# A joint Winograd level for one product of the gate and up projections, and sums of DFT blocks made by DMA

## The chip, the cores and the metric

The kernel runs on one core of a Trainium2 chip. The metric is the device time of one execution in microseconds. It is one launch; the arrays are laid out by the host beforehand and lie in HBM.

## What is computed

For x of 2048 rows and 512 columns, all in float32, the kernel mixes two branches:

```python
a = x @ hid_re.T;  b = x @ hid_im.T
y = seq_re @ a - seq_im @ b                  # Fourier mixing, real part
h = relu(x @ W_gate) * (x @ W_up)            # 512 -> 1792 columns
g = sigmoid(sum(x * gate_w, -1))
out = g * y + (1 - g) * (h @ W_down)
```

## The kernel before

**Arithmetic.** Every float32 operand is split into a high part `hi` and a low part `lo` of type float32r: ScalarE (ACT) makes `hi` by a cast, VectorE (DVE) makes `lo` by a subtraction. One product is three matmuls of 128x512 in PSUM: lo x hi, hi x lo, hi x hi (`PARTS`, line 366). Above that, matrix products are taken as 2x2 blocks with seven products instead of eight (Winograd). `LEFT` and `RIGHT` (lines 25, 26) name for each product 1 to 7 the blocks or sums that it multiplies: product 1 is block 11 by block 11, product 2 is block 12 by block 21. The eight PSUM banks are four pairs x, m, y, t, and `BANK` (line 29) says to which pair each product adds up.

**Gate and up.** W_gate and W_up are taken in seven column pairs c = 0 to 6, the rows of x in two halves q = 0, 1. One `Block` (line 493) is one c and one q: seven products, each for gate and up (i = 0, 1), each of 2 x 3 matmuls, 84 in all. After product 1 ACT copies pair x to pair y (line 542), so that both sums go on from it; products 5 and 6 are copied to SBUF as `s5`, `s6` (line 544); after products 2, 7, 3 and 4 the four blocks of h are finished on ACT and DVE (`rectified`, `added`, lines 528 to 539). `h_out` (line 474) makes the four sums of h that the down projection needs (`hs`) and stores h and the sums to `hd` in HBM.

**Order of the stages.** The blocks of c = 0 and 1 for q = 0 are interleaved at the start, product by product (lines 1006 to 1017; product 1 and 2 of the first block only are cut into shorter steps). Then come c = 2 to 6 with both halves, the spectral stage (x times the hidden DFT, results to `ad`), two remaining blocks of q = 1, `Down` (the down projection, twice), `Sequence` and `Joint` (the sequence DFT). `Joint` makes, for one of the two DFT matrices, products whose right sides are sums of DFT blocks; `joint_sums` (line 934) has made these ahead: each of its four calls loads four blocks of 512 KB (`jt`) on SyncE's DMA queue (SP), adds them pairwise on DVE (128x1024), and stores four results to `td` in HBM on GpSimd's queue (POOL).

**What sets the order.** Each operation is given a key, the number of matmuls planned ahead of it. `Plan` (line 129) works out when each is due and when its inputs are ready by its own table of costs, and lists DVE, ACT, SP and POOL in that order; TensorE (PE) keeps the written order. Each engine then runs its list in order. Loads go through SP; stores, and DMAs that add to their destination (`accumulate`), through POOL. SBUF is 51 equal units that buffers take in turn, so the first writer of a buffer waits for the last reader of the one before in its unit, a DMA included.

Of the kernel before, what the change touches and what calls it, by code (L numbers as in the profile page):

```python
# [14 lines left out]
P = 128  # L15
# [263 lines left out]
def kernel(ctx: ExitStack, tc, xP, xG, wgu, wd, cr, ci, wri, gw, out):  # L279
# [80 lines left out]
    def store(o, i):  # L360
        plan.gpsimd.dma_start(out=o, in_=i)

    def accumulate(o, i):
        plan.gpsimd.dma_start(out=o, in_=i, accum_op=OP.add)
# [9 lines left out]
    def x_load(q, b, ks=slice(0, 2), at=None):  # L374
        k, j = int(b[0]) - 1, int(b[1]) - 1
        (at or load)(piece[q, b][:, ks], xP[2 * q + j, k, :, ks])
# [6 lines left out]
    def x_sum(q, m):  # L383
        if len(RIGHT[m]) > 1:
            a, b = ((piece[q, n] if isinstance(n, str) else X[q, n][2]).all for n in RIGHT[m][:2])
            combine(X[q, m][2].all, a, b, RIGHT[m][2])
# [7 lines left out]
    def x_prep(q, m, key):  # L394
        x_raw(q, m)
        op(key, x_sum, q, m)
        op(key + 7, hi_of, X[q, m])
        op(key + 12, lo_of, X[q, m])
# [75 lines left out]
    def h_out(q, c, h, key):  # L474
        f = [buf(f"hs{n}") for n in range(2)]

        def first():
            e = E()
            e.vector.tensor_add(f[0][:, 0], h[0][:, 0], h[0][:, 1])
            e.vector.tensor_add(f[0][:, 1], h[0][:, 1], h[1][:, 1])  # L480

        def second():
            e = E()
            e.vector.tensor_add(f[1][:, 0], f[0][:, 0], h[1][:, 1])
            e.vector.tensor_add(f[1][:, 1], f[1][:, 0], h[1][:, 0])

        op(key, first)
        op(key + 6, second)
        op(key + 2, lambda: store(hd[q, 0, :, c], h[0][:, 0]))
        for n, t, k in ((1, h[1], 3), (3, f[0], 8), (5, f[1], 14)):  # L490
            op(key + k, lambda n=n, t=t: store(hd[q, n:n + 2, :, c].rearrange("x p n -> p x n"), t.all))

    class Block:


        def __init__(self, q, w, banks=PAIRS):
            self.q, self.w, self.banks = q, w, banks
            self.g = {r: buf("g" + r, (N,)) for r in ("11", "21")}
# [11 lines left out]
        def done(self, key):  # L510
            h_out(self.q, self.w.c, self.h, key)
# [6 lines left out]
        def one(self, m, i, k, n, first=0):  # L518
            w, x, ps = self.w.of(m, i, k), X[self.q, m], self.banks[BANK[m]]
# [4 lines left out]
        def evac(self, m, key):  # L524
# [11 lines left out]
            def added(r, ps, s):  # L536
                u, h = self.u[r], self.h[int(r[0]) - 1][:, 1]
                op(key, lambda: e.vector.tensor_add(u.all, ps.all, s.all))
                op(key + 1, lambda: e.vector.scalar_tensor_tensor(h, u[:, 0], 0.0, u[:, 1], op0=OP.max, op1=OP.mult))
# [12 lines left out]
            elif m == 4:  # L552
                rectified("21", 0, t, -1.0)

# [59 lines left out]
    class SpectralBlock:  # L614
        def __init__(self, sp, q, ih):
            self.sp, self.q, self.ih = sp, q, ih
            self.s = {m: buf(f"s{m}") for m in (5, 6)}
# [8 lines left out]
        def product(self, m, i):  # L626
            x, w, ps = X[self.q, m], self.sp.w[m], PAIRS[BANK[m]]
# [215 lines left out]
    class Joint:  # L843


        HI, LO = 31, 24
# [40 lines left out]
        def right(self, x, hh, key):  # L887
# [9 lines left out]
            op(key - 90, read)  # L897
# [64 lines left out]
    def x_half(m, k, hi=None):  # L962
        h, l, raw = (t[:, k] for t in X[0, m])
# [8 lines left out]
    for k in halves:  # L972
        op(-99, x_load, 0, "11", k)
        op(-99, ws[0].load, 0, halves[0], k)
    op(-99, ws[1].load, 0, halves[0])
    op(-99, x_load, 0, "21")
    for w in ws:
        op(-99, w.load, 0, halves[1])
    op(-98, x_load, 0, "12")
    for w in ws:  # L980
        op(-98, w.load, 1)
    op(-98, x_load, 0, "22")
    op(-98, lambda: load(gwt[:], gw))
    for k in halves:
        op(-90, x_half, 1, k, plan.vector.tensor_copy)
        op(-90, w_half, ws[0], halves[0], k)
    op(-90, w_half, ws[1], halves[0])
    op(-90, x_half, 2, halves[0])
    op(-90, w_half, ws[0], halves[1])
    op(-90, x_half, 2, halves[1])  # L990
    op(-90, w_half, ws[1], halves[1])
    for n, m in enumerate((5, 6, 3, 7, 4)):
        key = 24 * n + 20
        for f, *a in ((x_sum, 0, m), (hi_of, X[0, m]), (lo_of, X[0, m])):
# [12 lines left out]
    for m in ORDER_S:  # L1007
        for b in start:
            if m in (1, 2) and b is start[0]:
# [8 lines left out]
    for b in start:  # L1018
        b.done(plan.now + 100)
# [27 lines left out]

    blocks(sequence)
# [104 lines left out]
```

## Time and profile before

| | us |
|---|---|
| median of the runs (lowest, highest) | 790.61 (789.64, 792.07) |
| profiled execution | 789.88 |
| its span, first to last instruction | 788.1 |
| outside the span | 1.8 |
| PE busy, 3435 matmuls | 780.7 |
| DVE busy | 620.4 |
| ACT busy | 390.4 |
| POOL busy | 96.1 |

PE here is TensorE's matmuls, PEld its weight loads. The granted clock of TensorE was 0.999 over the span. In the chain of the work that ended last, each row is a start, a length and the instructions that ran in that time; in the list of waits the numbers are the total, how often, and the longest. Of a DMA, busy time counts only the issue, and "landing" is the time from issue until the data are there.

### The profile page before, as it was taken

How to read it: one execution, taken by the hardware profiler on the slowest of the kernel's cores; microseconds unless marked ns; L12 is line 12 of the kernel's file. 1: busy time of each engine (PE TensorE's matmuls, PEld its weight loads, DVE VectorE, ACT ScalarE, POOL GpSimd, SP SyncE). 2: the span in 40 equal slices, each digit the busy share in tenths (PEclk: the TensorE clock that was granted, in tenths of full speed). 3: DMA queues.
4: the chain of work that ended last, by engine and by line, in shares of the span. 5: the costliest groups of instructions: out<-in, count | busy, mean ns of one | idle time of the engine just before them, and what ended most of it. 6: DMA issues, size and time to landing. Idle time of an engine off the chain costs nothing.

```text
span 788.1 us, 9404 instructions
## 1 busy us (share of the span) xinstructions
PE 780.7 (99%) x3435; PEld 644.7 (82%) x3435; DVE 620.4 (79%) x663; ACT 390.4 (50%) x436; POOL 96.1 (12%) x142
## 2 busy tenths in 40 slices
PE   9999999999999999999999999999999999999997
PEld 7888888888888888888888888888888888888885
DVE  7999676667688314978764899967999999989963
ACT  6664333333354335476545464545757365574540
POOL 0011221212122111110000000200020001000200
PEclk9999999999999999999999999999999999999999
DMA  8354775576867975477688798859999889799914
GB/s 324 128 202 166 290 291 214 218 262 242 282 225 233 364 314 184 131 257 293 191 267 315 279 306 311 196 184 294 355 328 270 252 255 188 197 351 330 240 30 81
DMA packets 56574, 193.84 MB, mean 246 GB/s; under 512 B 6608, under 2 KB 6864, under 8 KB 56528
## 3 DMA queue, kind: packets, MB, share of 16 engines
q1 hardware_dynamic: 37552, 124.55, 45.2%
q0 software_dynamic: 18976, 68.69, 29.6%
q8 instruction: 27, 0.44, 0.2%
q14 instruction: 19, 0.16, 0.1%
HBM read 123.99 MB, written 60.83 MB: 235 GB/s over the span
## 4 chain that ended last, share of the span: by engine, by line
PE 97%; ACT 1%; issue 1%; DMA 1%; DVE 0%; SPq 0%; DVEq 0%
PE ps L126 97%; ACT jch L126 1%; DMA wr<-wgu 1%; SPq L126 0%; DVE v L126 0%; DVE z L126 0%; ACT js L126 0%; DVE wal L126 0%; ACT wah L126 0%; ACT ps L126 0%; DVEq L126 0%
## 5 line engine op out<-in xcount | busy, mean ns | idle before, releaser
L126 PE MATMUL ps<-ch,ll 128*128 128x512 f32 x580 | 225.6, 389 | 0.0
L126 PE MATMUL ps<-cl,lh 128*128 128x512 f32 x580 | 225.6, 389 | 0.0
L126 PE MATMUL ps<-ch,lh 128*128 128x512 f32 x580 | 225.6, 389 | 0.0
L126 ACT CAST ch<-r 128x1024 fp32r<-128x1024 f32 x96 | 97.4, 1052 | 72.5 <-DVE r L126 59.9
L126 PEld LDWEIGHTS ps<-ch,lh 128*128 128x128 f32 x580 | 108.9, 188 | 22.7
L126 PEld LDWEIGHTS ps<-ch,ll 128*128 128x128 f32 x580 | 108.9, 188 | 22.7
L126 PEld LDWEIGHTS ps<-cl,lh 128*128 128x128 f32 x580 | 108.9, 188 | 22.4
L126 DVE TENSOR_TENSOR cl<-r,ch 128x1024 fp32r<-128x1024 f32 x96 | 114.6, 1222 | 1.2 <-ACT ch L126 0.6
L126 ACT ACTIVATE ps<-ps 128x1024 f32<-128x1024 f32 (+1 forms) x34 | 32.6, 958 | 87.5 <-PE ps L126 41.0
L126 DVE TENSOR_TENSOR cl<-hr,ch 128x1024 fp32r<-128x1024 f32 (+1 forms) x56 | 59.3, 1088 | 20.4 <-ACT ch L126 18.6
L126 ACT COPY s<-ps 128x1024 f32<-128x1024 f32 x44 | 44.6, 1014 | 52.8 <-PE ps L126 52.8
L126 ACT CAST ch<-hr 128x1024 fp32r<-128x1024 f32 (+1 forms) x56 | 51.3, 942 | 26.7 <-PE ps L126 20.1
L126 DVE TENSOR_TENSOR r<-r,r 128x1024 f32<-128x1024 f32 x48 | 57.2, 1221 | 0.0
L126 POOL DMA_DIRECT2D out<-z x23 | 17.1, 743 | 322.5 <-DVE z L126 322.5
L126 DVE TENSOR_TENSOR u<-ps,s 128x1024 f32<-128x1024 f32 x28 | 34.2, 1221 | 12.4 <-PE ps L126 6.9
L126 PE MATMUL ps<-xh,wb0l 128*128 128x512 f32 x112 | 43.8, 391 | 0.0
L126 PE MATMUL ps<-xl,wb0h 128*128 128x512 f32 x112 | 43.6, 389 | 0.0
L126 PE MATMUL ps<-xh,wb0h 128*128 128x512 f32 x112 | 43.6, 389 | 0.0
L126 PE MATMUL ps<-xh,wb1h 128*128 128x512 f32 x112 | 43.6, 389 | 0.0
L126 PE MATMUL ps<-vh,xh 128*128 128x512 f32 x112 | 43.6, 389 | 0.0
L126 PE MATMUL ps<-vh,xl 128*128 128x512 f32 x112 | 43.6, 389 | 0.0
L126 PE MATMUL ps<-xh,wb1l 128*128 128x512 f32 x112 | 43.6, 389 | 0.0
(126 smaller groups left out, 1311.2 us busy)
## 6 DMA issues: line engine op xcount, KB each, us to landing
hr<-hd SPq DMA_DIRECT2D x42, 512.0 KB, 4.5
r<-cr SPq DMA_DIRECT2D x32, 512.0 KB, 5.7
r<-ci SPq DMA_DIRECT2D x32, 512.0 KB, 5.8
hd<-hs POOLq DMA_DIRECT2D x28, 512.0 KB, 5.2
out<-z POOLq DMA_DIRECT2D x23, 512.0 KB, 6.4
td<-jt POOLq DMA_DIRECT2D x16, 512.0 KB, 3.9
ad<-a POOLq DMA_DIRECT2D x16, 512.0 KB, 3.9
l<-ad SPq DMA_DIRECT2D x16, 512.0 KB, 7.2
```

Of the source, the lines that this page charges most:

```text
L126: getattr(getattr(nc, self.engine), self.name)(*map(ap, self.a), **{k: ap(x) for k, x in self.k.items()})
```

## The change

**Product 2 for both halves together.** For c = 3 to 6, a `Joined` pair of blocks replaces two Blocks. Block 12 of the weights and block 21 of x for both halves form a 2x2 product again, gate and up on one side, the two halves on the other. `JointW` and `JointX` make its sums, splits and seven steps of three matmuls: 21 in place of 24. `JointX` is prepared once (seven casts, eleven DVE operations of 128x512), `JointW` once per pair (four DVE operations of 128x128, a cast and a subtraction of 128x512). The steps run in pair x inside the q = 0 block, and their results reach SBUF as `jv` (ACT copies) and `jo` (DVE adds, one ACT copy), 128x512 each. For that, product 1 of the q = 0 block goes to pair y and is copied to `s1`, and the block "11" of h is made from `s1` or pair x plus `jo` by DVE (`u11`).

**Sums by DMA.** `joint_sums` makes the sums without SBUF: POOL copies a block from HBM into `td` in HBM and then adds a second block by an accumulating DMA. Two of the four sums start from a sum already in `td`. All 32 DMAs have 512 KB in pieces of 1 KB.

**Further edits.** At the start, products 1 and 2 of both blocks are cut into the short steps. The sums of h for c = 0, 1, q = 0 are made in the spectral stage from a reloaded h (`h_late`), and block 21 of x is reloaded and split again for that stage. x of the second half is prepared at a spacing of 24 instead of 27, and the right sides of `Joint` are loaded, cast and split a little later.

The core of the diff:

```diff
-    def h_out(q, c, h, key):
+    def h_sums(q, c, h, key):
...
+        for n, t, k in ((3, f[0], 8), (5, f[1], 14)):
+            op(key + k, lambda n=n, t=t: store(h_forms(q, c, n), t.all))
+
+    def h_forms(q, c, n):
...
+    def h_out(q, c, h, key, sums=True):
+        if sums:
+            h_sums(q, c, h, key)
         op(key + 2, lambda: store(hd[q, 0, :, c], h[0][:, 0]))
-        for n, t, k in ((1, h[1], 3), (3, f[0], 8), (5, f[1], 14)):
-            op(key + k, lambda n=n, t=t: store(hd[q, n:n + 2, :, c].rearrange("x p n -> p x n"), t.all))
+        op(key + 3, lambda: store(h_forms(q, c, 1), h[1].all))
+        if not sums:
+            op(key + 2, lambda: store(hd[q, 3, :, c], h[0][:, 1]))
+
+    def h_late(q, c, key):
+        h = [buf(f"hk{d}") for d in range(2)]
+        for i, n in enumerate((0, 3)):
+            op(key - 20 + i, lambda i=i, n=n: load(h[0][:, i], hd[q, n, :, c]))
+        op(key - 18, lambda: load(h[1].all, h_forms(q, c, 1)))
+        h_sums(q, c, h, key)
...
+        def added(self, r, a, b, key):
+            u, h = self.u[r], self.h[int(r[0]) - 1][:, int(r[1]) - 1]
+            op(key, lambda: E().vector.tensor_add(u.all, a.all, b.all))
+            op(key + 1, lambda: E().vector.scalar_tensor_tensor(h, u[:, 0], 0.0, u[:, 1], op0=OP.max, op1=OP.mult))
+    class Joined(Block):
+        def __init__(self, q, w):
+            super().__init__(q, w)
+            self.u["11"] = buf("u11")
+            if not q:
+                self.s[1] = buf("s1")
+        def run(self, joint=None):
+            slots = {(1, 1): (5, 1), (6, 1): (6,), (3, 0): (3, 7), (3, 1): (2, 4)}
+            for m, i in (*((m, i) for m in ((1, 5) if self.q else (5, 1)) for i in range(2)), (6, 0), (6, 1), (3, 0), (7, 0), (7, 1), (3, 1), (4, 0), (4, 1)):
+                pe(6, self.product, m, i)
+                if i:
+                    self.evac(m, plan.now)
+                for y in slots.get((m, i), ()) if joint else ():
+                    joint.step(y)
+        def done(self, key, joint):
+            self.added("11", self.s[1] if self.q == 0 else self.banks["x"], joint.o[self.q], plan.now)
+            super().done(key)
+        def one(self, m, i, k, n):
+            w, x, ps = self.w.of(m, i, k), self.x[m], self.banks["y" if m == 1 and not self.q else BANK[m]]
+            a, b = PARTS[n]
+            mm(ps[i], w[a], x[b][:, k], start=m in FIRST and k == n == 0, stop=m in (3, 4) and k == 1 and n == 2)
+        def evac(self, m, key):
+            y, t = self.banks["y"], self.banks["t"]
+            if m == 1 and not self.q:
+                op(key, lambda: E().scalar.copy(self.s[1].all, y.all))
+            elif m == 7:
+                for i in range(2):
+                    op(key, lambda i=i: E().scalar.activation(t[i], y[i], AF.Copy, scale=-1.0))
+                self.added("22", y, self.s[5], key)
+            else:
+                super().evac(m, key)
+    class JointX:
+        def __init__(self, key):
+            a, b = (piece[q, "21"] for q in range(2))
+            raw = [buf(f"jx{n}") for n in range(2)]
+            t5, t6, t7, t4 = raw[0][:, 0], raw[0][:, 1], raw[1][:, 0], raw[1][:, 1]
+            self.x = {}
+            for n, (y, src, f) in enumerate((
+                    (1, a[:, 0], None), (5, t5, (b[:, 0], a[:, 0])), (6, t6, (b[:, 1], t5)), (3, b[:, 1], None),
+                    (7, t7, (b[:, 1], b[:, 0])), (2, a[:, 1], None), (4, t4, (a[:, 1], t6)))):
+                x = self.x[y] = buf(f"jx{y}", dtype=F32R)
+                if f:
+                    op(key + 16 * n, lambda src=src, f=f: combine(src, *f, -1))
+                op(key + 16 * n + 4, lambda x=x, src=src: E().scalar.copy(x[:, 0], src))
+                op(key + 16 * n + 8, lambda x=x, src=src: E().vector.tensor_sub(x[:, 1], src, f32(x[:, 0])))
+    class JointW:
+        def __init__(self, w, x, key):
+            self.w, self.x = w, x
+            raw, s = buf("jws", [4, P]), w.raw[0]
+            self.t = buf("jw", [2, 4, P], F32R)
+            self.s = {y: buf(f"jv{y}", (N,)) for y in (1, 5, 6)}
+            self.o = [buf(f"jo{q}") for q in range(2)]
+            op(key - 30, lambda: combine(raw[:, 0], s[:, 1, 0, 1], s[:, 1, 1, 1], 1))
+            op(key - 30, lambda: combine(raw[:, 2], s[:, 1, 0, 0], s[:, 1, 0, 1], -1))
+            op(key - 29, lambda: combine(raw[:, 1], raw[:, 0], s[:, 1, 0, 0], -1))
+            op(key - 28, lambda: combine(raw[:, 3], s[:, 1, 1, 0], raw[:, 1], -1))
+            op(key - 24, lambda: E().scalar.copy(self.t[:, 0], raw.all))
+            op(key - 20, lambda: E().vector.tensor_sub(self.t[:, 1], raw.all, f32(self.t[:, 0])))
+        def left(self, y, a):
+            if y in (1, 2, 4):
+                return self.w.a[a][:, 1, int(y > 1), int(y == 4)]
+            return self.t[:, a, {5: 0, 6: 1, 7: 2, 3: 3}[y]]
+        def step(self, y):
+            pe(3, self.product, y)
+            self.evac(y, plan.now)
+        def product(self, y):
+            for n, (a, b) in enumerate(PARTS):
+                mm(PAIRS["x"][int(y in (5, 3, 2))], self.left(y, a), self.x.x[y][:, b],
+                   start=y in (1, 5, 2) and n == 0, stop=n == 2)
+        def evac(self, y, key):
+            Y, M = (PAIRS["x"][n] for n in range(2))
+            s, o, e = self.s, self.o, E()
+            if y in (1, 5, 6):
+                op(key, lambda: e.scalar.copy(s[y].all, M if y == 5 else Y))
+            elif y == 4:
+                op(key, lambda: e.scalar.copy(o[0][:, 1], Y))
+            else:
+                q, i, ps, t = {3: (1, 0, M, 6), 7: (1, 1, Y, 5), 2: (0, 0, M, 1)}[y]
+                op(key, lambda: e.vector.tensor_add(o[q][:, i], ps, s[t].all))
...
-        HI, LO = 31, 24
+        HI, LO = 26, 20
...
-            op(key - 90, read)
+            op(key - 82, read)
...
-        r = {b: buf(f"jt{b}") for b in BLOCKS}
-        for n, b in enumerate(("11", "12", "22", "21")):
-            op(key + 8 * n, lambda b=b: load(r[b].all, (cr, ci)[m][2 * int(b[1]) - 2, 1, 2 * int(b[0]) - 2 + hh]))
-        for n, (o, i) in enumerate((("11", "12"), ("12", "22"), ("22", "11"), ("21", "22"))):
-            op(key + 40 + 8 * n, lambda o=o, i=i: combine(r[o].all, r[o].all, r[i].all, 1))
-            op(key + 46 + 8 * n, lambda o=o, n=n: store(td[m, n, hh], r[o].all))
+        def c(b):
+            return (cr, ci)[m][2 * int(b[1]) - 2, 1, 2 * int(b[0]) - 2 + hh]
+        for n, (o, first, second) in enumerate(((0, "11", "12"), (1, "12", "22"), (2, 0, "22"), (3, 2, "21"))):
+            op(key + 30 * n, lambda o=o, i=first: store(td[m, o, hh], c(i) if isinstance(i, str) else td[m, i, hh], max_dma_last_dim=2 * N))
+            op(key + 30 * n + 15, lambda o=o, i=second: accumulate(td[m, o, hh], c(i), max_dma_last_dim=2 * N))
...
-            if m in (1, 2) and b is start[0]:
+            if m in (1, 2):
...
-        b.done(plan.now + 100)
+        b.done(plan.now + 8, False)
...
-        joint_sums(n // 2, n % 2, 380 + 160 * n)
-    sequence = [(2, 0), (2, 1)]
-    sequence += [(c, q) for c in range(3, NP) for q in range(2)]
-    tail = [(1, 1), (0, 1)]
+        joint_sums(n // 2, n % 2, 300 + 150 * n)
     spectral = Spectral()
-    def blocks(sequence):
-        nonlocal w
-        for c, q in sequence:
-            if w.c != c:
-                w = Weights(c)
-                if c == 1:
-                    w.fetch(plan.now - 140)
-                else:
-                    w_prep(w, plan.now, 66 if c else 180)
-            if c == 2 and q == 0:
-                for b in ("22", "11", "12", "21"):
-                    x_piece(1, b)
-                    op(plan.now - 100, x_load, 1, b)
-                for n, m in enumerate(ORDER):
-                    x_prep(1, m, plan.now - 46 + 27 * n)
-            Block(q, w).run()
-    blocks(sequence)
+    def prepared(c, ahead=66):
+        w = Weights(c)
+        w_prep(w, plan.now, ahead)
+        return w
+    for c in range(2, NP):
+        w = prepared(c)
+        if c == 2:
+            for b in ("22", "11", "12", "21"):
+                x_piece(1, b)
+                op(plan.now - 100, x_load(1, b))
+            for n, m in enumerate(ORDER):
+                x_prep(1, m, plan.now - 46 + 24 * n)
+            jx = JointX(plan.now + 70)
+            for q in range(2):
+                Block(q, w).run()
+        else:
+            pair = [Joined(q, w) for q in range(2)]
+            joint = JointW(w, jx, plan.now)
+            for q, b in enumerate(pair):
+                b.run(None if q else joint)
+                b.done(plan.now + 8, joint)
+    for q in range(2):
+        x_piece(q, "21")
+        op(plan.now - 150 + 60 * q, x_load(q, "21"))
+        x_prep(q, 2, plan.now - 100 + 100 * q)
...
+    for c in range(2):
+        h_late(0, c, plan.now + 30 * c)
     lefts = [spectrum(f) for f in range(2)]
     for ih in range(2):
         SpectralBlock(spectral, 1, ih)
-    blocks(tail)
+    w = Weights(1)
+    w.fetch(plan.now - 140)
+    Block(1, w).run()
+    Block(1, prepared(0, 180)).run()```

What stands on the engines at the places that matter: first TensorE's list after the change, in the q = 0 block of c = 4. The last matmuls of product 1 (`xh1`, `wah`, into pair y), then the joint steps 5 and 1 (`jx5`, `jx1`, into pair x), then product 6, which writes pair y.

```order
MATMUL ps_76<-xl1_113,wah_975 128x512
MATMUL ps_76<-xh1_107,wah_975 128x512
MATMUL ps_76<-jx5_635,jw_986 128x512 x3
MATMUL ps_76<-jx1_538,wal_994 128x512
MATMUL ps_76<-jx1_538,wah_975 128x512 x2
MATMUL ps_76<-xh6_230,wb0l_1006 128x512
```

Before, product 5 with its twelve matmuls stood between product 1 and product 6; it now runs ahead of product 1, and six joint matmuls are in its place.

Second, ScalarE's list at the same block: before the change (the copy of x to y, then of products 5 and 6, then the rectified "11" and the negated copy of product 7), and

```order
COPY ps_76<-ps_76 128x1024
COPY s5_1060<-ps_76 128x1024
COPY s6_1078<-ps_76 128x1024
ACTIVATE g11_1086<-ps_76 128x512
ACTIVATE ps_76<-ps_76 128x1024
```

after it, ScalarE's list from the cast of this pair's last weights on:

```order
CAST wd_1055<-wr1_939 128x512
COPY s5_1074<-ps_76 128x1024
COPY s1_1098<-ps_76 128x1024
COPY jv5_1107<-ps_76 128x512
COPY jv1_1112<-ps_76 128x512
COPY s6_1125<-ps_76 128x1024
COPY jv6_1132<-ps_76 128x512
ACTIVATE ps_76<-ps_76 128x512 x2
COPY jo0_1180<-ps_76 128x512
```

The copy to `s1` stands directly behind that to `s5`; three copies of joint steps are new, and the negated copy is two of 128x512.

Third, POOL's list after the change, from the stores of c = 4 on (`hd<-h`, `hd<-hs`: h and its sums) to those of c = 5, q = 0, with the copies and accumulates to `td` between them. An accumulate waits until its copy has landed, and a copy from `td` until the accumulate that made its source has.

```order
DMA td_70<-td_70 512x256
DMA hd_68<-h0_1346 128x512
DMA hd_68<-hs0_1362 128x2x512
DMA hd_68<-hs1_1371 128x2x512
DMA td_70<-ci 512x256 x2
DMA td_70<-td_70 512x256
DMA hd_68<-h0_1469 128x512
DMA td_70<-ci 512x256
DMA hd_68<-h1_1451 128x2x512
DMA td_70<-ci 512x256
DMA hd_68<-hs0_1494 128x2x512
```

Before, stores of `jt`, which waited for DVE alone, stood in these places.

More of the change, by code (lines that the diff above doesn't have):

```diff
@@ L358, in load, with store, accumulate @@
         plan.sync.dma_start(o, i)
[L360 to L364, printed above, removed]
+    def store(o, i, **k):
+        plan.gpsimd.dma_start(out=o, in_=i, **k)
+    def accumulate(o, i, **k):
+        plan.gpsimd.dma_start(out=o, in_=i, accum_op=OP.add, **k)
     PARTS = ((1, 0), (0, 1), (0, 0))
@@ L383, in x_sum @@
     def x_sum(q, m):
-        if len(RIGHT[m]) > 1:
-            a, b = ((piece[q, n] if isinstance(n, str) else X[q, n][2]).all for n in RIGHT[m][:2])
-            combine(X[q, m][2].all, a, b, RIGHT[m][2])
+        o, i = X[q, m][2], [piece[q, n] if isinstance(n, str) else X[q, n][2] for n in RIGHT[m][:2]]
+        return lambda: len(i) == 1 or combine(o.all, i[0].all, i[1].all, RIGHT[m][2])
     def hi_of(t):
@@ L497, in __init__ @@
             self.q, self.w, self.banks = q, w, banks
+            self.x = {m: X[q, m] for m in ORDER if (q, m) in X}
             self.g = {r: buf("g" + r, (N,)) for r in ("11", "21")}
@@ L508, in run, with done @@
             self.done(plan.now + (8 if plan.now > 270 else 100))
-        def done(self, key):
-            h_out(self.q, self.w.c, self.h, key)
+        def done(self, key, *sums):
+            h_out(self.q, self.w.c, self.h, key, *sums)
         def product(self, m, i):
@@ L536, in added @@
             def added(r, ps, s):
-                u, h = self.u[r], self.h[int(r[0]) - 1][:, 1]
-                op(key, lambda: e.vector.tensor_add(u.all, ps.all, s.all))
-                op(key + 1, lambda: e.vector.scalar_tensor_tensor(h, u[:, 0], 0.0, u[:, 1], op0=OP.max, op1=OP.mult))
+                self.added(r, ps, s, key)
             if m == 1:
@@ L616, in __init__ @@
             self.sp, self.q, self.ih = sp, q, ih
+            self.x = {m: X[q, m] for m in ORDER}
             self.s = {m: buf(f"s{m}") for m in (5, 6)}
```

34 lines of the change are left out of this document (18 added, 16 removed).

## The prediction

> **What bounds the kernel now.** I read the page's first table, then the chain that ended last, then what TensorE (PE) waited for.
>
> ```profile
> span 788.1 us, 9404 instructions
> PE 780.7 (99%) x3435; PEld 644.7 (82%) x3435; DVE 620.4 (79%) x663; ACT 390.4 (50%) x436; POOL 96.1 (12%) x142
> ...
> PE 97%; ACT 1%; issue 1%; DMA 1%; DVE 0%; SPq 0%; DVEq 0%
> ```
>
> PE is busy for 780.7 of 788.1 us. A busy PE alone would not prove a bound, since each matmul's record overlaps the next one; the chain does. These are its long pieces (start, length, what):
>
> ```profile
> 8.16 542.15 PE ps L126 x2387
> ...
> 555.68 0.48 ACT js L126
> ...
> 556.21 144.24 PE ps L126 x635
> ...
> 706.36 75.11 PE ps L126 x330
> ```
>
> Three unbroken runs of matmuls make 761.5 us. In the first, 542.15 / 2387 = 0.227 us per 128x512 matmul. Between the runs stand only the two Joint stages. What PE waited for confirms it:
>
> ```profile
> PE ps L126 <- DVE warm L126: 1.2, 1, 1.2
> PE ps L126 <- ACT js L126: 0.5, 2, 0.3
> PE ps L126 <- DVE wal L126: 0.4, 1, 0.4
> ```
>
> So time is the number of matmuls times 0.227 us plus about 2 us of waits. Matmuls taken away pay in full, and work on the vector engine (DVE), ScalarE (ACT) or a DMA queue costs nothing until PE waits for it.
>
> **Term 1: matmuls removed.** Each of the pairs c = 3 to 6 made product 2 in 2 halves x 2 (gate, up) x 2 x 3 = 24 matmuls of 128x512; seven products of three make 21. Four pairs save 4 x 3 = 12, and 12 x 0.227 = **-2.72 us**. Everything else in the change can only add to this or take from it.
>
> **Term 2: the copy of product 1.** In a joined pair's q = 0 block, product 1 goes to bank pair y, ACT copies y to s1, and product 6 overwrites y. Between them stand the joint steps 5 and 1: six matmuls. The same kind of copy of product 1 in the kernel before, start, length and form:
>
> ```profile
> 103.83 0.39 PE L126 MATMUL ps<-xh,wah 128*128 128x512 f32 x1
> ...
> 104.25 1.00 ACT L126 COPY ps<-ps 128x1024 f32<-128x1024 f32 x1 [3.45 <-PE ps L126]
> ...
> 555.58 0.39 PE L126 MATMUL ps<-jch,jlh 128*128 128x512 f32 x1
> 555.59 1.05 ACT L126 COPY js<-ps 128x512 f32<-128x512 f32 x2
> ...
> 556.21 0.50 PE L126 MATMUL ps<-jch,jll 128*128 128x512 f32 x1 [0.25 <-ACT js L126]
> ...
> 556.55 0.40 PE L126 MATMUL ps<-jcl,jlh 128*128 128x512 f32 x1
> ```
>
> The copy begins 104.25 - 103.83 = 0.42 us after the last matmul starts, and one into SBUF takes 1.01 us (the s<-ps row below). How fast PE resumes is read from the js stall: by the chain the copy waited for ends at 555.68 + 0.48 = 556.16, PE starts at 556.21, and its next matmul follows 0.34 us later instead of 0.227, so resuming costs about 0.05 + 0.11 = 0.16. Needed: 0.42 + 1.01 + 0.16 = 1.59 us. Available: from the start of product 1's last matmul to product 6's first are seven steps, 7 x 0.227 = 1.59. The balance is zero, so I take **0**, if ACT is free when product 1 ends. ACT then has only the s5 copy behind it, twelve matmuls (2.7 us) earlier. Should a 1.05 us cast stand in front, each pair loses up to 1.05 us, 4.2 in all. Below zero it cannot go: nothing there waited before.
>
> ```profile
> L126 ACT CAST ch<-r 128x1024 fp32r<-128x1024 f32 x96 | 97.4, 1052 | 72.5 <-DVE r L126 59.9 <-PE ps L126 7.1 <-DVE ll L126 4.0
> ...
> L126 ACT COPY s<-ps 128x1024 f32<-128x1024 f32 x44 | 44.6, 1014 | 52.8 <-PE ps L126 52.8
> ```
>
> The later joint copies and adds are 128x512, 0.57 us (js: 1.05 for two) to 0.69 us (below), and the bank each frees is next written after at least 12 more matmuls, 2.7 us: hidden.
>
> **Term 3: DVE and ACT.** DVE is the only other engine that is ever full; busy time is its column, then that of ACT, in 20 us windows, the last columns the share of DMA and GB/s.
>
> ```profile
> 20.00:40.00 20.00, 20.00 (x90) 16.52 (x89) 19.84 (x26) 13.49 (x18) 2.28 (x5) 1.00 0.33 132
> 40.00:60.00 20.00, 20.00 (x90) 16.57 (x89) 19.32 (x22) 12.62 (x15) 2.86 (x5) 1.00 0.50 188
> 60.00:80.00 20.00, 20.00 (x90) 16.54 (x89) 19.05 (x25) 8.00 (x9) 3.39 (x5) 1.00 0.52 183
> 80.00:100.00 20.00, 20.00 (x90) 16.53 (x89) 13.66 (x19) 6.70 (x8) 4.81 (x7) 1.00 0.80 292
> ...
> 180.00:200.00 20.00, 20.00 (x90) 16.58 (x89) 14.30 (x19) 9.04 (x11) 3.44 (x6) 1.00 0.70 247
> ...
> 280.00:300.00 20.00, 20.00 (x89) 16.50 (x89) 2.66 (x4) 6.08 (x6) 2.85 (x4) 1.00 0.78 290
> ```
>
> ```profile
> L126 DVE TENSOR_TENSOR jt<-jt,jt 128x1024 f32<-128x1024 f32 x16 | 19.5, 1220 | 0.1
> ...
> L126 DVE TENSOR_TENSOR hs<-hs,h 128x512 f32<-128x512 f32 x28 | 19.1, 689 | 0.3
> ```
>
> From 40 to 100 us DVE has 19.32 + 19.05 + 13.66 = 52.0 us. The right sides of the joint product add 11 operations of 128x512, 7.6 us; the first joint weights one of 128x512 and four of 128x128, not over 5 x 0.69 = 3.4. The sums of the first two blocks leave (8 x 0.69 = 5.5), and so do four adds of jt (4 x 1.22 = 4.9). That is 52.6 of 60 us, so it still fits. In a steady pair (180 to 200: 14.30 of 20) about 4 us per 37 are added, and the removed adds give back up to 4.9. The late sums of the first blocks fall at 280 to 300, where DVE has 2.66 of 20. **0**. If this cover were gone, 1 us of DVE would be 1 us of PE.
>
> **Term 4: start.** At 8.16 us PE had waited 0.4 us for wal; the new order of products 1 and 2 puts both blocks' first halves ahead of the operand waited for, so this wait goes.
>
> ```profile
> 9.16 1.14 ACT L126 CAST xh<-x 128x512 fp32r<-128x512 f32 x2 [0.37 <-DMA x<-xP]
> ...
> 10.21 1.14 ACT L126 CAST wah<-wr 128x512 fp32r<-128x512 f32 x2
> ```
>
> But product 2 is next late: its x waits for a DMA and is cast at 9.16, its weights from 10.21 on, the first half done near 10.8. The loss moves there and nearly all of it stays: I take 0, from -0.6 (the wait and its slow restart) to +1.0 (the copy of block 1's product 1, 1.0 us, now stands before the cast of the second half).
>
> **Term 5: the Joint stages.** Each js stall costs 556.55 - 555.58 = 0.97 against two steps of 0.45: 0.5 us. Casts there now come five matmuls later, and one jch cast sits between the two js copies. Nearest rows: -0.5 each if the stall goes, +1.05 each if a cast comes in front. I take 0.
>
> **Term 6: the sums made by DMA.** No DMA from HBM to HBM is in this trace. The nearest rows (512 KB each; median to landing; and the spread of r<-r):
>
> ```profile
> hd<-hs POOLq DMA_DIRECT2D x28, 512.0 KB, 5.2
> out<-z POOLq DMA_DIRECT2D x23, 512.0 KB, 6.4
> td<-jt POOLq DMA_DIRECT2D x16, 512.0 KB, 3.9
> ...
> r<-r POOLq DMA_DIRECT2D x16, 512.0 KB, 8.8
> ```
>
> ```profile
> DMA to landing us min/median/max: 5.1/8.8/15.5
> ```
>
> A copy I put between td<-jt, which also writes td, and out<-z (stores and accumulates into HBM mixed), c = 3.9 to 6.4; I take 5.5, since it reads HBM as well. An accumulate I put between 5.1 and 15.5, a = 8.8, the median of r<-r, the nearest row though it adds from SBUF into SBUF, beside equally heavy traffic. The sums are read by jc<-td, whose row gives duration and then the first and last start:
>
> ```profile
> L126 SPq DMA_DIRECT2D jc<-td x16: 319/327/1127, 525.8 to 699.1; - x16
> ```
>
> That is some 300 us after the last is made, so their landing itself costs nothing; only what they hold up on POOL counts, and that is the second rival below. **0**. The Trainium skill (DMA: Bandwidth & Descriptors, section Anatomy of one DMA) fits 2.0 us plus the bytes at 436 GB/s, 3.2 us for 512 KB; by it POOL would never be late. The trace's 3.9 to 8.8 us for that size disagree, and the sum does not use it.
>
> **Sum.** 789.88 (the profiled execution; span 788.1 and 1.8 around it) - 2.72 = 787.16. That execution lies 0.73 under the median of the runs, 790.61; on the median the forecast is 787.89, **787.9 us**, -0.34%. A measurement of this kernel tells about 0.3%, 2.4 us, from no change, so the border is 788.2.
>
> **Rivals.**
> First, small waits give it back. s1 late by part of a cast in the four pairs (0 to 4.2 us), start up to 1.0, Joint up to 2.1. For it: s1's balance is exactly zero, and DVE is full until 80 us. Against: ACT is at 50%. Half a cast per pair gives 787.9 + 4 x 0.5 = **789.9**, within 0.3%.
>
> Second, POOL's queue stalls PE: slower. POOL issues in order, and an accumulate waits until its copy has landed, a second-stage copy until its source has. The h stores stand behind them, and their buffers are reused. The tightest is the store of hs0_1494: the copy of product 5 of c = 6 takes its buffer, and product 5 ends 842 matmuls after 8.16, at 199.1 us. Back from that store stand, each waiting for the one before, copies and accumulates from the copy at about 125 us (it follows the stores of c = 3, whose matmuls end at 8.16 + 500 x 0.227 = 121.6) with 4c + 3a between, then some 3 us of issues and the landing, 5.2. Landed at 125 + 4c + 3a + 8: at c = 5.5, a = 8.8 this is 181; the data exist near 184.5, so 190, and 9 us are to spare. It decides from 4c + 3a = 66: c = 6.4 with a = 13.5. At c = 6.4 and a = 15 it is 5 us late by this chain, and up to 17 if the first call's lag adds up: 793 to 805, say **797**. For it: 15.5 occurs in the trace, DMA is 0.70 busy there, an accumulate reads HBM twice, and pieces are small. Against: the median is 8.8.
>
> The Trainium skill (same page, Two DMAs through the same engine are not ordered) says that a dependent DMA must be held by its issuing engine until the first one's semaphore has come. The trace agrees in kind: for its accumulates POOL stood 4.9 us for the landing of r<-cr.
>
> ```profile
> L126 POOL DMA_DIRECT2D r<-r x16 | 13.5, 846 | 29.9 <-DVE cl L126 18.6 <-DMA r<-cr 4.9 <-PE ps L126 3.2
> ```
>
>
> Third, both small losses go: the start (-0.6) and the Joint stalls (-1.0): **786.3**.
>
> **How the numbers follow.** Forecast as summed, 0.48; third rival 0.05; together faster 0.53. First rival 0.27: same 0.25, and 0.02 over the border at 793.0. Second rival 0.20, slower with that: 0.22. The range goes from 786.4, just above the third rival, to 796, which takes in the near half of the second and leaves out its far half, about 0.1, and some 0.05 below.
>
> **What would show it.** Term 1: PE with 3423 instructions, and three long runs again of 0.227 us per matmul. Term 2: a PE wait on ACT s1 means the first rival. Term 3: a PE wait on DVE near 30 to 110 us. Term 4: waits before 16 us. Term 5: PE waits on js. Term 6: the landing of td<-td, td<-cr and td<-ci, and waits of ACT or DVE on hd<-hs between 90 and 240 us. I would be wrong if accumulates take more than about 13 us to land, or if PE waits at s1 in every pair.

## The result, and the profile after

The changed kernel takes 789.20 us (median of 20 runs, 788.09 to 791.51), the kernel before 790.38 (20 runs, 789.64 to 792.52): ratio 0.9984, 95% interval 0.9978 to 0.9990. That is 1.2 us less, not the 2.7 of the forecast. It is under the 0.3% that the prediction took as the border, but the interval, from 20 runs each, lies clear of 1. 789.20 lies inside the range; the case that came true is the first rival, small waits that give the gain back, which had been put at 0.27. The waits are in other places than the text had named. The profiled execution took 789.34 us, 0.54 under that of before (789.88).

The page's first lines and PE's waits, after:

```profile
span 787.6 us, 9450 instructions
PE 779.2 (99%) x3423; PEld 641.2 (81%) x3423; DVE 635.0 (81%) x700; ACT 403.6 (51%) x465; POOL 116.4 (15%) x160
```

```profile
PE ps L126 <- DVE warm L126: 1.2, 1, 1.2
PE ps L126 <- ACT s L126: 0.7, 1, 0.7
PE ps L126 <- ACT wah L126: 0.6, 1, 0.6
PE ps L126 <- DVE u L126: 0.5, 1, 0.5
```

The twelve matmuls are gone (3423 for 3435). The js waits have left the list, `wah` stands in place of `wal`, and `s` and `u` are new. The list counts only idle time, and a matmul that resumes is slow besides (0.34 us to the next start instead of 0.227), so I set the matmuls' starts in the timeline against an even step of 0.2268 us, and summed what exceeds it:

| stage (matmul number) | before | after |
|---|---|---|
| start (14 to 120) | 1.49 | 1.51 |
| first joined pair begins, 82 us (345 to 360) | 0.00 | 0.77 |
| the joined pairs otherwise (360 to 1020) | 0.07 | 0.72 |
| blocks to spectral stage, 244 us (1020 to 1110) | -0.01 | 1.22 |
| the two Joint stages | 1.09 | 0.72 |
| everything else | -0.24 | -0.32 |
| sum | 2.40 | 4.62 |

The sum grows by 2.22, and 2.22 - 12 x 0.2268 = -0.50 us, against a difference of -0.54 between the two executions. So the gain was paid in full, and 2.22 us of waits took most of it. Three of them are read here, and the start further below.

At 82 us, DVE's rows and then PE's (start, length):

```profile
78.02 1.23 DVE L126 TENSOR_TENSOR u<-ps,s 128x1024 f32<-128x1024 f32 x1 [1.05 <-ACT ps L126]
79.16 0.28 DVE L126 TENSOR_TENSOR jws<-jws,wr 128x128 f32<-128x128 f32 x1
79.36 0.28 DVE L126 TENSOR_TENSOR jws<-wr 128x128 f32<-128x128 f32 x1
79.56 0.28 DVE L126 TENSOR_TENSOR jws<-wr,jws 128x128 f32<-128x128 f32 x1
79.77 0.68 DVE L126 TENSOR_TENSOR h<-g,ps 128x512 f32<-128x512 f32 x1
80.36 0.69 DVE L126 TENSOR_TENSOR ws<-wr,wr 128x512 f32<-128x512 f32 x1
80.97 0.69 DVE L126 TENSOR_TENSOR jw<-jws,jw 128x512 fp32r<-128x512 f32 x1
81.57 1.22 DVE L126 TENSOR_TENSOR u<-ps,s 128x1024 f32<-128x1024 f32 x1
```

```profile
82.00 0.39 PE L126 MATMUL ps<-xh,wd 128*128 128x512 f32 x1
82.84 0.50 PE L126 MATMUL ps<-xh,wb0l 128*128 128x512 f32 x1 [0.46 <-DVE u L126]
```

The last `u` frees pair m, which product 5 of the first joined block overwrites. A joined block begins with product 5, so only product 4's twelve matmuls cover this `u`; a plain block begins with product 1 and covers it with 24. Six operations stand between the two `u`, five of them for the new weights.

At 244 us, DVE, ACT and PE, and what DVE waited for:

```profile
232.89 2.35 DVE L126 TENSOR_TENSOR u<-ps,s 128x1024 f32<-128x1024 f32 x2 [2.43 <-DMA hd<-h]
...
242.73 1.22 DVE L126 TENSOR_TENSOR xl<-x,xh 128x1024 fp32r<-128x1024 f32 x1
...
244.06 1.01 ACT L126 COPY s<-ps 128x1024 f32<-128x1024 f32 x1 [3.98 <-DVE xl L126]
```

```profile
244.06 0.39 PE L126 MATMUL ps<-vh,xh 128*128 128x512 f32 x1
245.12 0.50 PE L126 MATMUL ps<-vh,xl 128*128 128x512 f32 x1 [0.68 <-ACT s L126]
```

The copy `s` (s6 of the first spectral block) takes the buffer that held block 21 of the second half of x, reloaded by the change, and must wait until DVE has made `xl` from it. DVE comes to that late: 2.43 us of its lag is a wait for a store of h to land. This place takes 0.95 of the 1.22 us; most of the rest (0.23) is lost at the next weights, `vl`, which DVE also makes late.

At 188 us, in the second block of c = 5, the copy of s6 has six matmuls (half of product 3) before product 7 overwrites its bank pair:

```profile
187.14 0.39 PE L126 MATMUL ps<-xh,wb0h 128*128 128x512 f32 x1
...
187.88 1.01 ACT L126 COPY s<-ps 128x1024 f32<-128x1024 f32 x1 [0.56 <-ACT jw L126]
...
188.95 0.50 PE L126 MATMUL ps<-xh,wb1l 128*128 128x512 f32 x1
```

It starts 0.74 us after the last matmul instead of 0.42, and PE loses those 0.3 us. Why it starts late is open: the profile names the cast of `jw` ahead of it, but that had ended at 187.32.

### The profile page after: what moved, and what is told of

The parts are those of the page before. It is cut to its first block, busy times and chain, and to the rows that moved or that the text cites. A ratio compares the mean times of both kernels' runs of the same rounds, so it can differ in the third digit from the quotient of the medians.

```text
span 787.6 us, 9450 instructions
## 1 busy us (share of the span) xinstructions
PE 779.2 (99%) x3423; PEld 641.2 (81%) x3423; DVE 635.0 (81%) x700; ACT 403.6 (51%) x465; POOL 116.4 (15%) x160
## 4 chain that ended last, share of the span: by engine, by line
PE 84%; DMA 6%; issue 5%; DVE 2%; POOL 2%; ACT 1%; SPq 0%; POOLq 0%; ACTq 0%; DVEq 0%
PE ps L126 84%; DMA td<-ci 3%; DMA hd<-hs 2%; DMA td<-td 2%; POOL td L126 1%; POOL hd L126 1%; DVE u L126 1%; DVE h L126 1%; DMA wr<-wgu 0%; DVE hs L126 0%; ACT jch L126 0%; DVE v L126 0%; DVE z L126 0%; DVE vl L126 0%; DVE xl L126 0%
## 5 line engine op out<-in xcount | busy, mean ns | idle before, releaser
L126 PE MATMUL ps<-ch,ll 128*128 128x512 f32 x580 | 225.6, 389 | 0.0
L126 PE MATMUL ps<-cl,lh 128*128 128x512 f32 x580 | 225.6, 389 | 0.0
L126 PE MATMUL ps<-ch,lh 128*128 128x512 f32 x580 | 225.6, 389 | 0.0
L126 ACT CAST ch<-r 128x1024 fp32r<-128x1024 f32 x96 | 97.2, 1051 | 63.2 <-DVE r L126 52.6
L126 PEld LDWEIGHTS ps<-cl,lh 128*128 128x128 f32 x580 | 108.9, 188 | 22.7
L126 PEld LDWEIGHTS ps<-ch,ll 128*128 128x128 f32 x580 | 108.9, 188 | 22.6
L126 PEld LDWEIGHTS ps<-ch,lh 128*128 128x128 f32 x580 | 108.9, 188 | 22.5
L126 DVE TENSOR_TENSOR cl<-r,ch 128x1024 fp32r<-128x1024 f32 x96 | 114.6, 1219 | 2.4 <-ACT ch L126 2.0
L126 ACT COPY s<-ps 128x1024 f32<-128x1024 f32 x48 | 48.8, 1016 | 65.6 <-PE ps L126 59.4
L126 ACT ACTIVATE ps<-ps 128x1024 f32<-128x1024 f32 (+1 forms) x42 | 33.8, 805 | 89.0 <-PE ps L126 59.5
L126 DVE TENSOR_TENSOR cl<-hr,ch 128x1024 fp32r<-128x1024 f32 (+1 forms) x56 | 59.5, 1087 | 18.4 <-ACT ch L126 16.5
L126 ACT CAST ch<-hr 128x1024 fp32r<-128x1024 f32 (+1 forms) x56 | 51.4, 944 | 27.3 <-PE ps L126 19.7
L126 POOL DMA_DIRECT2D out<-z x23 | 17.0, 739 | 316.2 <-DVE z L126 310.9
L126 DVE TENSOR_TENSOR r<-r,r 128x1024 f32<-128x1024 f32 x48 | 57.1, 1218 | 0.0
L126 PE MATMUL ps<-xh,wb0l 128*128 128x512 f32 x112 | 44.0, 393 | 0.5 <-DVE u L126 0.5
L126 PE MATMUL ps<-vh,xl 128*128 128x512 f32 x112 | 43.7, 390 | 0.7 <-ACT s L126 0.7
L126 PE MATMUL ps<-xh,wb1l 128*128 128x512 f32 x112 | 43.9, 392 | 0.1
L126 PE MATMUL ps<-vl,xh 128*128 128x512 f32 x112 | 43.7, 390 | 0.0
L126 PE MATMUL ps<-xl,wb0h 128*128 128x512 f32 x112 | 43.6, 389 | 0.0
L126 PE MATMUL ps<-xh,wb0h 128*128 128x512 f32 x112 | 43.6, 389 | 0.0
L126 PE MATMUL ps<-vh,xh 128*128 128x512 f32 x112 | 43.6, 389 | 0.0
L126 PE MATMUL ps<-xl,wb1h 128*128 128x512 f32 x112 | 43.6, 389 | 0.0
## 6 DMA issues: line engine op xcount, KB each, us to landing
hr<-hd SPq DMA_DIRECT2D x42, 512.0 KB, 4.5
r<-cr SPq DMA_DIRECT2D x32, 512.0 KB, 6.8
r<-ci SPq DMA_DIRECT2D x32, 512.0 KB, 8.2
hd<-hs POOLq DMA_DIRECT2D x28, 512.0 KB, 8.8
out<-z POOLq DMA_DIRECT2D x23, 512.0 KB, 6.6
ad<-a POOLq DMA_DIRECT2D x16, 512.0 KB, 8.4
l<-ad SPq DMA_DIRECT2D x16, 512.0 KB, 8.0
r<-r POOLq DMA_DIRECT2D x16, 512.0 KB, 7.8
```

Of the source, the lines that this page charges most:

```text
L126: getattr(getattr(nc, self.engine), self.name)(*map(ap, self.a), **{k: ap(x) for k, x in self.k.items()})
```

## The experiments

Theory U: the wait at 82 us is u12, the `u` of block 12 of h, standing behind other DVE work. Theory Q: POOL's queue, with accumulates that wait for landings, causes the wait at 244 us. Theory V: DVE's backlog there causes it. Theory C: too little cover for the copy of s6. Theory J: the later casts shortened the Joint waits. Ratios are to the kernel before on the same chip, with 95% intervals; the changed kernel stands at 0.9984. Losses are sums over matmul starts in the profiled execution, as in the table.

**e1: sums by DVE as before.** `joint_sums` and its keys as in the kernel before.

> The changed kernel, but the right-side sums of the Joint stages are made as before: loads into SBUF by SP, adds on DVE (16 x 1.22 us), stores by POOL. Theory Q (POOL's queue: accumulates that wait for landings hold up the stores of h, and DVE and ACT then wait for their buffers; 0.34 us lost at 188 us and about 1.2 us at 244 us in the profile): these waits vanish, no landing of hd<-hs over 10 us before 250 us, and the time falls by about 1.4 us against the changed kernel, to 0.9967 of the kernel before. Theory V (the losses come from a fuller DVE): the adds return to DVE, the waits stay or grow, and the time is not under that of the changed kernel, 0.9984 or more.

Measured 792.92, 1.0033 (1.0022 to 1.0044): slower. The `u` wait stays (0.76), and at the change of stage PE loses 3.42 us, although POOL no longer waits for landings in td:

```profile
247.71 0.50 PE L126 MATMUL ps<-vh,xl 128*128 128x512 f32 x1
250.20 0.50 PE L126 MATMUL ps<-vl,xh 128*128 128x512 f32 x1 [1.99 <-DVE vl L126]
```

Theory Q's forecast for it failed.

**e2: the kernel before with only the sums by DMA.**

```diff
-        joint_sums(n // 2, n % 2, 380 + 160 * n)
+        joint_sums(n // 2, n % 2, 300 + 150 * n)
```

> The kernel before with one part of the change: the right-side sums made by HBM-to-HBM copies and accumulates on POOL's queue, at the keys of the changed kernel. Theory Q: the h stores are held up here as well; landings of td<-ci near 9.5 us, PE loses 0.5 to 1.5 us between 180 and 250 us, ratio 1.0006 to 1.002. Theory V: DVE is relieved of 19.5 us and nothing waits, ratio 0.999 to 1.000.

Measured 790.62, 1.0004 (0.9996 to 1.0013): nothing. POOL waits here as much as in the changed kernel,

```profile
POOL td L126 <- DMA td<-td: 30.8, 4, 10.7
...
POOL td L126 <- DMA td<-ci: 29.2, 6, 9.6
```

with 14.6 us more for td<-cr, and PE loses nothing between 120 and 550 us. Waits on POOL alone do not reach PE; 19.5 us less on DVE gains nothing either.

**e3: no joint product.** Two plain blocks in each of the four pairs.

> The changed kernel with plain blocks for c = 3 to 6, product 2 of each half by itself: 12 matmuls more. If the joint product pays 12 x 0.227 = 2.72 us in full and costs nothing, the time is 2.7 us over the changed kernel, ratio 1.0018. If the joint product itself brings waits (0.73 us at 82 us, where PE waited for u12), these go and the ratio is 1.0005 to 1.001; theory Q expects the wait at 244 us to stay.

Measured 793.65, 1.0045 (1.0030 to 1.0061). The wait at 82 us is gone, but 5.95 us are lost at the change of stage, most of them behind a `u` of DVE and the slow matmuls after it, so that the total says nothing of the joint product's own worth. Inconclusive for its purpose; the slow matmuls are read under the hardware below.

**e4: the four calls of the sums side by side**, each DMA about 96 matmuls behind the one that it needs.

```diff
+            step = 96 // len(each)
...
+                op(key + step * n, lambda ...: store(td[m, o, hh], ...))
+                op(key + 96 + step * n, lambda ...: accumulate(td[m, o, hh], ...))
+            key += 192
```

> The changed kernel with the same 32 DMAs for the sums, same bytes, but the four calls side by side: eight copies, then the eight accumulates, four copies, and so on, each about 22 us of matmuls behind the DMA that it depends on, so that POOL has nothing to wait for. Theory Q: POOL's waits for td landings (67 us in the profile) fall under 10 us, the waits at 188 and 244 us vanish, time 1.4 us under the changed kernel, ratio 0.9967. Theory D (the DMA engines are busier with the same bytes moved twice, whatever the order): the landings of hd<-hs stay near 9 us and the ratio stays at 0.9984.

Measured 794.10, 1.0046 (1.0033 to 1.0059). POOL's waits for td fell to some 10 us as meant, and the time rose. At the change of stage 1.36 us were lost, this time behind `vl`, and a new loss of 4.5 us came at 120 us behind DVE's `wb0l`, 1.6 of it in slow matmuls. Landings got worse (td<-ci 12.9 us). Theory Q's forecast failed again, but the worse landings leave it a way out; e7 closes that. Theory D, which the expectation names, had the time unchanged and failed as well.

**e5: weights of the first joined pair 24 matmuls earlier.**

```diff
+        w = prepared(c, 90 if c == 3 else 66)
...
+            joint = JointW(w, jx, plan.now - (24 if c == 3 else 0))
```

> The changed kernel; the weights of the first joined pair (c = 3) are loaded, summed and split 24 matmuls earlier, so that in DVE's list four operations fewer stand between u22 and u12 of c = 2. Theory U (PE's wait of 0.73 us at 82 us is u12 standing behind DVE work, with only product 4's 12 matmuls to hide it since product 5 now opens the next block): the wait goes, the time falls by 0.7 us against the changed kernel, the wait at 244 us stays near 1.2 us. Rival: DVE as a whole is behind here, and the wait stays or only moves.

Measured 788.42, 0.9979 (0.9970 to 0.9988). The wait at 82 us is gone (0.77 to 0.00), in this and in the profiles of all later runs with the edit; in the six profiles of the joint product without it, it is 0.75 to 0.78. Only two operations now stand between the two `u`. The first begins at 78.09, and then come:

```profile
79.23 0.68 DVE L126 TENSOR_TENSOR h<-g,ps 128x512 f32<-128x512 f32 x1
79.82 0.69 DVE L126 TENSOR_TENSOR ws<-wr,ws 128x512 f32<-128x512 f32 x1
80.42 1.22 DVE L126 TENSOR_TENSOR u<-ps,s 128x1024 f32<-128x1024 f32 x1
```

Theory U holds. In the profiled execution (787.71) the wait at 244 us was absent too, but the runs reach from 787.42 to 790.10, so it seems to come in some and not in others.

**e6: block 21 of the second half reloaded and split later.**

```diff
+        op(plan.now - 150 + 180 * q, x_load(q, "21"))
+        x_prep(q, 2, plan.now - 100 + 200 * q)
```

> The changed kernel; block 21 of the second half of x is reloaded and split some 100 matmuls later, out of the change of stage at 244 us. Theory V (the wait there is DVE's backlog at the change of stage, to which xl of 1.22 us and the buffer it keeps belong): the copy s6 no longer waits for xl, the wait of 1.0 us vanishes or falls under 0.3, time about 1 us under the changed kernel; POOL's waits for td landings stay near 67 us. Theory Q (POOL's queue holds up the h stores): the wait stays near 1 us, since the landing waits of DVE before it (2.4 us on hd<-h) stay.

Measured 788.26, 0.9976 (0.9966 to 0.9985). The copy no longer waits for `xl`. At the change of stage 0.68 us are lost in the profiled execution, more than V asked for; most of it is at another place, a copy from pair x to y at 239 us. That execution was the slowest of nine (789.11; the others 788.02 to 788.55). The runs spread over 1.1 us, those of e5 on the same chip over 2.7. POOL's waits for td stayed, 67 us.

**e7: both edits.**

> Both edits together, the earlier weights of c = 3 and the later block 21. If the losses at 82 and 244 us add up and nothing else took the gain of the 12 matmuls: 1.9 us under the changed kernel, ratio 0.996. If one of them only hides another wait: 0.997 or more.

Measured 787.86, 0.9968 (0.9956 to 0.9981); runs 787.57 to 788.26. Neither loss is left (0.00 and -0.01), while POOL waits for td longer than ever, 81 us. With that theory Q falls.

**e8: the planner told that DMAs from HBM to HBM land 3 us later.**

```diff
+                if all(x.base.kind == "dram" for x in (*s.writes, *s.reads)):
+                    s.end += 3.0
```

> The changed kernel, with the planner told that a DMA from HBM to HBM lands 3.0 us later than it had assumed (the trace has 7.2 us for copies and 9.5 for accumulates), so that it lists the stores of h ahead of the accumulates that still wait. Theory Q: POOL's waits for td fall from 67 us to under 40, DVE's wait for hd<-h (2.4 us near 231 us) goes, and with it the PE wait at 244 us; time 1 us under the changed kernel. Theory V: POOL's waits fall, but the PE wait at 244 us stays and the time is that of the changed kernel within 0.5 us.

Measured 791.05, 1.0013 (1.0004 to 1.0022). POOL's waits fell to 55 us, the loss at the change of stage grew to 3.78, 1.6 of it in slow matmuls, and PE now lost time before two more joined pairs (158 and 196 us). Neither theory had this: a truer cost in one place reordered the lists elsewhere.

**e9: both halves of product 3 ahead of product 7 in the second block.**

```diff
+            mid = ((3, 0), (3, 1), (7, 0), (7, 1)) if self.q else ((3, 0), (7, 0), (7, 1), (3, 1))
```

> The changed kernel; in the second block of a joined pair both halves of product 3 run before product 7, so that twelve matmuls instead of six stand between product 6 and product 7 and cover the copy of s6. Theory C (a copy of 1.01 us needs 0.42 + 1.01 + 0.16 = 1.59 us, exactly six matmuls and a step, so any cast in front of it shows; 0.36 us lost near 188 us and 0.25 between 115 and 185 us): these losses go, time 0.4 to 0.5 us under the changed kernel. Rival: the wait moves to the copies into pair t, which now have only six matmuls before product 4, and nothing is gained.

Measured 789.14, 0.9991 (0.9979 to 1.0003): not told apart from the changed kernel by time, since 1.20 us are still lost at the change of stage, and the runs spread from 787.67 to 792.11. Here most of the loss is behind `vl`, although the copy `s` waited for `xl` as before:

```profile
247.69 0.50 PE L126 MATMUL ps<-vl,xh 128*128 128x512 f32 x1 [0.68 <-DVE vl L126]
```

So the lateness of DVE's list reaches PE at more than one place. In e9's profile the losses at s6 are nearly gone (0.36 to 0.00; 360 to 800: 0.27 to 0.04). Theory C holds by the profile.

**e10: all three edits.**

> The earlier weights of c = 3, the later block 21 and the order of the second block together. If the three losses are independent: 0.5 us under the kernel with two edits (787.86), ratio about 0.996. If the new order upsets the lists elsewhere: 787.9 or more.

Measured 787.08, 0.9962 (0.9949 to 0.9975): the fastest kernel here, 0.8 us under e7, although the two intervals overlap. The loss at 188 us is gone here as well.

**e11: e7 with the Joint casts at the old distances.**

```diff
+        HI, LO = 31, 24
...
+            op(key - 90, read)
```

> The kernel with the two edits (earlier weights, later block 21), but the right sides of the Joint stages cast and loaded at the old distances (31, 24, 90). Theory J (the later casts leave ACT free for the js copy; the two Joint waits fell from 0.54 to 0.36 us each): both waits return to 0.54 and the time is 0.35 us over that kernel. Rival: the waits fell for the removal of the jt adds or by chance, and they stay at 0.36.

Measured 788.30, 0.9974 (0.9965 to 0.9983). Both js waits are back (0.56 and 0.57, from 0.36):

```profile
553.87 0.39 PE L126 MATMUL ps<-jch,jlh 128*128 128x512 f32 x1
553.90 1.05 ACT L126 COPY js<-ps 128x512 f32<-128x512 f32 x2
...
554.52 0.50 PE L126 MATMUL ps<-jch,jll 128*128 128x512 f32 x1 [0.27 <-ACT js L126]
```

In the changed kernel the step to the next matmul is 0.45 (555.43 to 555.88). Theory J holds; it is worth 0.4 us by the account of starts. The removal of the adds of jt, its rival, is out as well: e2 has no such adds and the old distances, and loses 0.56 at each Joint stage.

**e12: e7 with the sums by DVE.**

> The kernel with the two edits, but the sums of the Joint stages made on DVE as before the change. Theory V (with the joint product DVE has no room at the change of stage near 240 us, so its 19.5 us of adds must go elsewhere): PE loses 1 to 3 us between 235 and 255 us again, time 1 to 3 us over that kernel, ratio 0.998 to 1.001. Rival: with block 21 out of the way DVE has room, and the time stays at 0.997; then the sums by DMA were not needed.

Measured 787.50, 0.9967 (0.9954 to 0.9979), the same as e7. DVE is full for 30 us, and PE loses nothing (behind the window and its length stand the busy times of the matmuls, the weight loads and DVE):

```profile
210.00:220.00 10.00, 10.00 (x46) 8.29 (x45) 9.97 (x11) 3.70 (x5) 2.04 (x4) 1.00 0.98 358
220.00:230.00 10.00, 10.00 (x46) 8.12 (x45) 9.88 (x12) 5.21 (x7) 2.86 (x5) 1.00 0.93 342
230.00:240.00 10.00, 10.00 (x46) 8.29 (x45) 10.00 (x12) 4.48 (x6) 0.71 (x1) 1.00 0.43 150
```

So a full DVE is not by itself the cause at 244 us, and theory V as put falls as well. What is left is narrower: the order of DVE's list and who holds the buffer. With block 21 later and the weights earlier, the loss is absent in four profiles of four (e7, e10, e11, e12). It also means that with these two edits the sums by DMA bring nothing that can be measured: 787.50 without them, 787.86 with them.

## Why the prediction was right and wrong

**Term 1, -2.72: right.** 12 matmuls fewer, 0.2268 us each, and the account of both executions closes with it. In e10, where the losses sum to 2.24 against 2.40 before, the profiled execution (786.97) is 2.91 us under that of before.

**Term 2, 0: right, and the balance was as close as worked out.** At the four copies to s1 the starts exceed the even step by 0.02 us each. In e7 a cast came in front of one of them, and it cost 0.23. (A detail was wrong without harm: the bank of joint step 6 is next written after nine matmuls, not "at least 12".)

**Term 3, 0: this step failed.** It said that "it still fits" because DVE had 52.6 us of work in 60. DVE did have that room on average, but the loss at 82 us is one operation, u12, in the wrong place of the list (0.77, shown by e5). The prediction weighed the bank of each joint copy and the sums of busy time, but it missed that beginning a block with product 5 halves the cover of the `u` before it, and that the new order of the second block leaves s6's copy only six matmuls (0.55 in four pairs, shown by the profiles of e9 and e10). It also left out the reloaded block 21; at 244 us that held a buffer that the copy of s6 needed. The loss there was 1.22 in the profile. That it varies from execution to execution is argued from the spreads of kernels run together, 2.7 us in e5 and 0.7 in e7, 4.4 in e9 and 0.7 in e10; the kernel before, which has no such loss in its profile, spread over 2.9 us beside e9 and e10, so this is not shown. How much of the loss is the late landing of h and how much the order of the list was not separated.

**Term 4, 0: right in its size, not in its place.** 1.49 before, 1.51 after. The wait for `wal` went, but the loss did not move to product 2: only 0.11 lies at its first matmul. Half of it (0.75) lies at the first matmuls of product 1, whose weights landed later in this execution, so that ACT cast them at 4.72 and not at 4.18 as before:

```profile
4.72 0.40 ACT L126 CAST wah<-wr 128x256 fp32r<-128x256 f32 x1 [2.70 <-DMA wr<-wgu]
...
5.17 0.74 PE L126 MATMUL ps<-xh,wah 128*128 128x512 f32 x2 [0.58 <-ACT wah L126]
```

In e11, with the same start, 1.19 us lie at product 2. Over its twelve profiles the new start costs 1.21 to 1.91, the old one 1.49 and 1.11 in its two, so that two equal sizes are in part luck.

**Term 5, 0: inside its bounds.** The two stages gained 0.37 together, by the casts' distances (e11, e2).

**Term 6, 0: right, with dearer DMAs than taken.** In the changed kernel:

```profile
hd<-hs POOLq DMA_DIRECT2D x28, 512.0 KB, 8.8
...
td<-cr POOLq DMA_DIRECT2D x12, 512.0 KB, 7.2
td<-ci POOLq DMA_DIRECT2D x12, 512.0 KB, 9.5
...
td<-td POOLq DMA_DIRECT2D x8, 512.0 KB, 7.2
```

td<-td are copies, the other two four copies and eight accumulates each. With c = 7.2 and a = 9.5 (the dearer of the two mixed rows), 4c + 3a = 57 stays under the 66 from which the second rival was to decide, and PE lost nothing at the beginning of c = 6. POOL waited 67 us for td, and e2 shows the like without cost. The Trainium skill's fit (DMA: Bandwidth & Descriptors, Anatomy of one DMA), 3.2 us by estimate, is far from the 7.2.

**The rivals.** The first came true in its size, 1.5 us given back by the medians (2.2 in the profiled executions) against 2.0 forecast, but by other waits than the three named. That the size came near is luck: it was worked out from casts in front of s1, and s1 cost 0.02 us. The chance for the likeliest case was too high: it took five terms as zero, and of the covers behind them only that of s1 was worked out.

## What to carry to other kernels

When an edit moves a step of the bounding engine, work out the cover of every copy around it, not of the new ones only: for each bank, matmuls between its last write and the next, times their step, against latency, copy and restart (here 0.42 + 1.01 + 0.16 = 1.59 us, or six matmuls between the two). A cover that fits exactly is thin: it cost 0.02 us each time at s1, but 0.07 at s6 in three pairs and 0.34 in the fourth. Average room on another engine says little; what counts is which operation stands ahead of the one that is waited for, and whose buffer it needs. A change of 0.3% is judged from the account of starts in the profile, and then by repairing each loss by itself: here that turned -0.16% into -0.38%.

## What the runs showed of the hardware

**Half speed after a pause.** In e3 PE stood still for some 3.3 us, resumed, and 1.5 us later ran seven matmuls at 0.427 us and one at 0.402:

```profile
237.38 0.39 PE L126 MATMUL ps<-vh,xh 128*128 128x512 f32 x1
240.92 0.50 PE L126 MATMUL ps<-vh,xl 128*128 128x512 f32 x1 [3.15 <-DVE u L126]
...
242.44 0.63 PE L126 MATMUL ps<-vh,xl 128*128 128x512 f32 x1
242.87 0.63 PE L126 MATMUL ps<-vl,xh 128*128 128x512 f32 x1
...
245.43 0.57 PE L126 MATMUL ps<-vl,xh 128*128 128x512 f32 x1
```

The granted clock shows it (the number after POOL's):

```profile
240.00:245.00 5.00, 4.08 (x13) 3.21 (x13) 5.00 (x7) 1.96 (x2) 0.00 (x0) 0.74 0.12 47
```

From 242.44 to 245.83 are 3.4 us, and some 8 x 0.20 = 1.6 us are lost on top of the pause. e4 did the same after a step of 3.04 us between two starts, e1 did not after one of 2.49. e8 did it after two shorter steps on end, of 0.65 and 1.89 us, so the length of one pause does not decide:

```profile
248.38 0.50 PE L126 MATMUL ps<-vh,xl 128*128 128x512 f32 x1 [0.26 <-ACT vh L126]
250.27 0.50 PE L126 MATMUL ps<-vl,xh 128*128 128x512 f32 x1 [1.38 <-DVE vl L126]
...
251.42 0.63 PE L126 MATMUL ps<-vh,xh 128*128 128x512 f32 x1
251.85 0.63 PE L126 MATMUL ps<-vh,xl 128*128 128x512 f32 x1
```

The Trainium skill (TensorE: Matmul & The Clock Gate, HAM oscillation) names pauses over about 3.4 us; in e4 one of 3.04, less the matmul's own 0.23, was enough.

**DMAs from HBM to HBM** of 512 KB took 4.8 to 11.7 us to land in the changed kernel (median 8.1), against a median of 3.9 for the store from SBUF before; side by side (e4) the medians for td<-cr and td<-ci rose to 11.1 and 12.9.
